# Spectral matrices in their own tiles loaded ahead, two row tiles, and early expert slots taken from three places of the list

## The chip, the cores and the metric

One core of a Trainium2 chip runs the kernel. The metric is the device time of one execution in microseconds (us). Of the kernel before there are three runs, 3310.20, 3313.72 and 3321.25 us; their median is 3313.72 us. Another execution was taken with a profile, 3312.02 us, and every row below is of that one.

## The reference

Eight sequences of 3072 tokens with 256 channels pass a spectral filter, a feed-forward block that takes the largest of three projections, and a mixture of eight experts of which each token uses one. [...]

```python
X = np.fft.rfft(x, axis=1)
x = np.fft.irfft(X * F, n=3072, axis=1).reshape(8 * 3072, 256)
h = np.maximum(np.maximum(x @ w1, x @ w2), x @ w3)          # 768 wide
x = h @ w_out
logits = normalize(x) @ normalize(expert_emb).T / tau        # 8 experts
e = argmax(logits); g = softmax(logits)[e]
out[token] = g * (relu(x[token] @ moe2_w1[e]) @ moe2_w2[e])  # 1024 wide
```

Counted with the reference from its own inputs, experts 0 to 7 get 6555, 2627, 10962, 295, 744, 233, 3084 and 76 tokens. In groups of 256, rounded up, that is 26, 11, 43, 2, 3, 1, 13 and 1, in all 100. From the first seven sequences alone, rounded down, it is 22, 8, 37, 1, 2, 0, 10 and 0, in all 80.

## The kernel before, in words

**Three stretches.** The first (to about 124 us) does the spectral filter of sequence 0 as a pass of its own (`whole`), while the weights of the feed-forward block are decoded from 64-bit words. The second (to about 2118 us) walks 48 units `u` of 512 tokens, six to a sequence. Each unit has 18 ticks `pt`; in each tick TensorE does one group of six 512-column matmuls (`f_group`, tile `p`), in ticks 3 to 6 also the second projection of the unit before (`x2_tile`, tile `pso`), and `fill` puts a piece of the next sequences' spectral passes between them, as a planner with due points says. The third stretch (from 2118 us) does the experts: 100 slots of 256 tokens (`SURE`), one after the other, some 11.45 us each.

**A spectral pass** (class `Pass`) has a stage A, which transforms along one factor and writes to memory, and a stage B of steps `i`. Step `i` consists of two pieces. `b1` loads (`z_load`, `b_load`, on SyncE's queue), splits the input of the next step (`b_split`) and multiplies (`b_fwd`, tile `psb`); `b2` mixes and multiplies back (`b_inv` of step i-3, in the whole pass i-2, tile `psi`). One tile `bt` holds both matrices of a step, forward and inverse, and is kept until `b_inv` has used it; there are five. The filter values `ft` have two tiles, the inputs `x` four. One tick after `b_fwd`, VectorE does the shuffle `t` and the product `u`, and a tick later GpSimd multiplies `t` by the filter.

**Row tiles.** `x2_tile` writes unit u-1's result into one tile `r` (pool `r_p`, one buffer); `x2_store` sends it to memory from SyncE's queue in tick 17, after the last step of `route2` has written the gate into it (L600). `route3` scatters the token numbers into one list per expert (GpSimd, L639).

**Expert slots.** `tables` works out on VectorE which list row each slot takes: `tables(0, 12, ...)` for the first 12 slots (`EARLY`) in unit 43, from the first seven sequences, and `tables(12, ...)` for the rest in the third stretch. Three buffers hold expert weights; slot s uses buffer s modulo 3, and each buffer walks a contiguous run of the list (`_runs`). `w_load(s, i)` (GpSimd's queue, L990) gathers half i of a slot's weights, 2 MB; if the slot's expert is the one that the buffer already holds, its row numbers are out of bounds and nothing is moved. Buffer 2 lies in `wt`, the feed-forward weights, and comes free with the last `f_group`. A slot's tokens are gathered by GpSimd (`x_load`, `xg`), turned by SyncE (`x_turn`, DMA transposes, `xw`), and spread and split on ScalarE and VectorE (`x_split`: L1055, L1056, L204, L205, `xT`).

Of the kernel before, what the change touches and what calls it, by code (L numbers as in the profile page):

```python
# [10 lines left out]
F32 = mybir.dt.float32  # L11
F32R = mybir.dt.float32r
# [11 lines left out]
E, FF = 8, 1024  # L24
# [17 lines left out]
RELEASE = 18 * 38  # L42
NW = 3
# [70 lines left out]
def _runs(n):  # L114

    at = np.arange(128)
    size = (n + NW - 1 - np.arange(NW)) // NW
    start = np.cumsum(size) - size
    return np.where(at < n, start[at % NW] + at // NW, at)

# [6 lines left out]
def _layout(inputs):  # L127
# [11 lines left out]
    c32 = np.zeros((128, 160), np.float32)  # L139
# [5 lines left out]
    c32[:, 26:26 + 128] = np.arange(128)  # L145
    c32[:, 154] = _runs(EARLY)
    c32[:, 155] = _runs(SURE - EARLY)
# [6 lines left out]
        "b32": np.stack([b, bi], 2).astype(np.float32),  # L154
# [15 lines left out]
def fft_filter_maxout_moe_kernel(ctx: ExitStack, tc: tile.TileContext, I, out):  # L170
# [20 lines left out]
    c32 = const.tile([128, 160], F32, name="c32")  # L191
# [4 lines left out]
    pidx, sgn, iotas = c32[:, 24:25], c32[:, 25:26], c32[:, 26:26 + 128]  # L196
    runs = c32[:, 154:155], c32[:, 155:156]
# [9 lines left out]
    def body():  # L207
        st = ExitStack()
        with st:
            def mk(name, bufs, **kw):  # L210
# [7 lines left out]
            b_p, f_p, x_p, xs_p, o_p, u_p, t_p, ys_p = (  # L218
                fft.enter_context(tc.tile_pool(name=n, bufs=b))
                for n, b in (("b", 5), ("f", 2), ("x", 4), ("xs", 3), ("o", 3), ("u", 3), ("t", 3), ("ys", 4))  # L220
# [24 lines left out]
            class Pass:  # L245
# [69 lines left out]
                def b_load(self, i):  # L315
                    if not 0 <= i < self.nb:
                        return
                    if self.whole:
                        bt = b_p.tile([96, 2, 2, 96], F32, tag="b", name="bt")
                        sp.dma_start(out=bt, in_=I["b32"][2 * i:2 * i + 2].rearrange("g p m o -> p g (m o)"))  # L320
                        ft = f_p.tile([96, 2, 2, D], F32, tag="f", name="ft")
                        sp.dma_start(out=ft, in_=I["filt"][2 * i:2 * i + 2].rearrange("g p m o -> p g (m o)"))
                    else:
                        bt = b_p.tile([96, 4, 96], F32R, tag="b", name="bt")
                        sp.dma_start(out=bt.bitcast(F32), in_=bmd[i // 4][i % 4])
                        ft = f_p.tile([96, 1, 2, D], F32, tag="f", name="ft")
                        sp.dma_start(out=ft[:, 0], in_=I["filt"][i])
                    self.t["b", i] = bt
                    self.t["f", i] = ft
# [544 lines left out]

            slot = {}
            cols = {}

# [392 lines left out]
```

## Time and profile before

| what | us |
|---|---|
| median of three runs | 3313.72 |
| the profiled execution | 3312.02 |
| its span, first to last instruction | 3310.1 |
| TensorE matmul busy in the span | 3186.3 |
| VectorE, ScalarE, GpSimd busy | 1916.9, 1527.8, 1245.5 |
| mean granted TensorE clock | 0.98 of full |

The span is 1.9 us shorter than the execution's own time. A row of instructions reads: start, duration (both in us), engine, line, operation, output<-input, count, and in brackets the idle time before it with what ended it. SPq and POOLq are the parts of SyncE and GpSimd that issue. A waits row reads: engine, line, <- what it waited for: us in all, times, longest. A window row reads: stretch, its length, then for PE, PEld, DVE, ACT and POOL the busy time with the count of instructions, the granted clock, the busy share of the DMA engines and GB/s.

### The profile page before, as it was taken

Reading aid. Unit: us, or ns where it says so; the run is one execution under the profiler, and the core shown is the slowest. Engines: PE = TensorE matmul, PEld = TensorE weight load, DVE = VectorE, ACT = ScalarE, POOL = GpSimd, SP = SyncE. Lnnn points to the kernel's source line nnn. Section 1 sums busy time; section 2 is a strip of 40 time slices with the busy share of each in tenths; the row PEclk is TensorE's granted clock in tenths of the full one; section 3 lists DMA queues with packets and bytes.
Section 4 is the critical chain, followed back from the end, with each engine's and each line's share of the span. In section 5 each row is a group of like instructions: output and inputs, shape, how many; then the busy total and the mean of one; then the engine's idle time right before and its main releaser. Section 6 shows DMA issues by size and latency. Waiting matters only on the chain.

```text
span 3310.1 us, 56666 instructions
## 1 busy us (share of the span) xinstructions
PE 3186.3 (96%) x20524; PEld 2858.4 (86%) x20524; DVE 1916.9 (58%) x4249; ACT 1527.8 (46%) x3450; POOL 1245.5 (38%) x1294
## 2 busy tenths in 40 slices
PE   5799999999999999999999999998999999999998
PEld 2588878878788888888888888998999999999998
DVE  7778687677788756878646775542333333333332
ACT  3545545545554554454445554433433333333333
POOL 3233233232233322333322223354555554555553
PEclk6999999999999999999999999999999999999999
DMA  8756566466564452444206777345333457422433
GB/s 247 236 135 141 128 136 138 123 118 151 153 124 101 102 131 89 98 103 98 60 26 174 228 225 216 75 84 160 71 70 69 120 119 186 98 71 70 115 73 93
DMA packets 326911, 409.83 MB, mean 124 GB/s; under 512 B 165784, under 2 KB 234787, under 8 KB 323428
## 3 DMA queue, kind: packets, MB, share of 16 engines
q1 hardware_dynamic: 230324, 247.87, 32.7%
q0 software_dynamic: 55088, 107.96, 11.4%
q10 hardware_dynamic: 41216, 50.35, 4.8%
q8 instruction: 164, 2.69, 0.4%
q14 instruction: 119, 0.97, 0.1%
HBM read 613.68 MB, written 140.97 MB: 228 GB/s over the span
## 4 chain that ended last, share of the span: by engine, by line
PE 55%; issue 19%; POOL 13%; DMA 7%; DVE 4%; ACT 1%; POOLq 1%; SPq 0%; ACTq 0%; DVEq 0%
PE p L201 32%; PE pso L201 13%; POOL out L1099 4%; POOL xg L1035 4%; POOL w L990 4%; PE psi L201 2%; PE psb L201 2%; DMA bt<-bmd 2%; PE psy L201 2%; PE psa L201 2%; POOL wt L990 2%; DMA ft<-in_filt 1%; DMA xw<-xg 1%; DMA s<-ot 1%; PE psh L201 1%
## 5 line engine op out<-in xcount | busy, mean ns | idle before, releaser
L201 PE MATMUL p<-y,wt 128*128 128x512 f32 x5184 | 1322.7, 399 | 1.6 <-DVE m L512 1.0
L201 PEld LDWEIGHTS p<-y,wt 128*128 128x128 f32 x5184 | 954.1, 190 | 206.5 <-DVE m L512 1.5
L1078 DVE SCALAR_TENSOR_TENSOR h<-psh,h 128x512 fp32r<-128x512 f32 x400 | 275.4, 689 | 459.6 <-ACT h L1077 458.0
L201 PEld LDWEIGHTS pso<-wo,h 128*128 128x128 f32 x3456 | 448.6, 189 | 20.4 <-ACT m L508 3.1
L201 PE MATMUL pso<-wo,h 128*128 128x264 f32 x3456 | 454.7, 285 | 2.6 <-ACT m L508 2.6
L201 PE MATMUL psh<-xT,w 128*128 128x256 f32 x3216 | 418.0, 285 | 7.0 <-ACT xT L204 6.6
L201 PEld LDWEIGHTS psh<-xT,w 128*128 128x128 f32 x3216 | 401.8, 193 | 8.0 <-ACT xT L204 7.0
L201 PE MATMUL pso<-w,h 128*128 128x256 f32 x3216 | 407.9, 283 | 0.6 <-ACT o L1094 0.6
L368 POOL TENSOR_TENSOR t<-t,ft 96x256 f32<-96x256 f32 (+1 forms) x176 | 178.3, 1013 | 584.0 <-DVE t L364 285.0
L201 PEld LDWEIGHTS pso<-w,h 128*128 128x128 f32 x3216 | 395.7, 192 | 0.8 <-ACT o L1094 0.8
L1099 POOL DMA_INDIRECT out<-o,ti x200 | 201.8, 1009 | 438.7 <-ACT o L1094 419.7
L1077 ACT ACTIVATE h<-psh 128x512 fp32r<-128x512 f32 x400 | 237.1, 593 | 268.6 <-PE psh L201 268.6
L639 POOL DMA_INDIRECT lst<-ids,pi x192 | 215.1, 1120 | 330.5 <-DVE gs L242 135.7
L486 POOL TENSOR_TENSOR y<-df,sm 128x256 fp32r<-128x256 f32 x192 | 153.1, 798 | 486.8 <-DVE df L485 485.8
L1094 ACT ACTIVATE o<-pso,gate 128x256 f32<-128x256 f32 x200 | 94.8, 474 | 423.3 <-PE pso L201 416.5
L241 ACT ACTIVATE h<-m 128x512 fp32r<-128x512 f32 x288 | 181.4, 630 | 208.9 <-DVE m L516 199.6
L516 DVE TENSOR_TENSOR m<-p,m 128x512 f32<-128x512 f32 x288 | 197.4, 686 | 93.7 <-PE p L201 91.0
L242 DVE TENSOR_TENSOR h<-m,h 128x512 fp32r<-128x512 f32 x288 | 210.0, 729 | 67.1 <-ACT h L241 66.2
L512 DVE TENSOR_TENSOR m<-p,m 128x512 f32<-128x512 f32 x288 | 197.0, 684 | 75.7 <-PE p L201 73.4
L542 ACT COPY r<-pso 128x512 uint16<-128x512 uint16 x192 | 112.5, 586 | 262.9 <-PE pso L201 262.9
L205 DVE TENSOR_TENSOR xT<-xf,xT 128x512 fp32r<-128x512 f32 x100 | 69.3, 693 | 281.6 <-ACT xT L204 278.9
L1035 POOL DMA_INDIRECT xg<-x2d,ti x200 | 208.0, 1040 | 63.9 <-issue 62.8
(158 smaller groups left out, 4199.2 us busy)
## 6 DMA issues: line engine op xcount, KB each, us to landing
wsd<-wsp SPq DMA_DIRECT2D x32, 1024.0 KB, 9.4
ft<-in_filt SPq DMA_DIRECT2D x160, 192.0 KB, 4.5
x2d<-r SPq DMA_DIRECT2D x48, 514.0 KB, 3.3
xt<-in_x SPq DMA_DIRECT2D x96, 256.0 KB, 4.4
s<-ot ACTq DMA_DIRECT2D x96, 256.0 KB, 3.4
gt<-s SPq DMA_DIRECT2D x94, 256.0 KB, 5.0
bt<-bmd SPq DMA_DIRECT2D x160, 144.0 KB, 3.5
raw<-in_e SPq DMA_DIRECT2D x32, 512.0 KB, 6.7
```

The source lines that it names most:

```text
L201: pe.matmul(out=o, lhsT=l, rhs=r, start=start, stop=stop)
L241: act.activation(out=hi, in_=src, func=ACTF.Copy)
L242: later(1, lambda: dve.tensor_tensor(out=lo, in0=src, in1=hi.bitcast(F32), op=ALU.subtract))
L368: later(1, lambda: pool.tensor_tensor(out=t, in0=t, in1=fb, op=ALU.mult))
L512: dve.tensor_tensor(out=m2, in0=ps, in1=m_t[u, fc], op=ALU.max)
L516: dve.tensor_tensor(out=m2, in0=ps, in1=m2, op=ALU.max)
L639: s = pool.indirect_dma_start(out=lst1, out_offset=bass.IndirectOffsetOnAxis(ap=pi[:, t:t + 1], axis=0), in_=ids[:, t:t + 1], in_offset=No ...
L990: pool.indirect_dma_start(out=ws[s % NW][i].bitcast(F32), out_offset=None, in_=wsd[i], in_offset=bass.IndirectOffsetOnAxis(ap=cols["wi"][: ...
L1035: pool.indirect_dma_start(out=g[:, t], out_offset=None, in_=x2d[0:n], in_offset=bass.IndirectOffsetOnAxis(ap=slot[s][:, t], axis=0), bound ...
L1077: act.activation(out=h[:, 0], in_=ps, func=ACTF.Relu)
L1078: dve.scalar_tensor_tensor(out=h[:, 1], in0=ps, scalar=0.0, in1=h[:, 0].bitcast(F32), op0=ALU.max, op1=ALU.subtract,)
L1099: d = pool.indirect_dma_start(out=out, out_offset=bass.IndirectOffsetOnAxis(ap=slot[s][:, t], axis=0), in_=o[:, t], in_offset=None, bounds ...
```

## The change

- **Matrices.** `b_load` becomes `m_load(i, m)` with one tile per matrix: three tiles for forward matrices, loaded two steps ahead, and four for inverse ones, loaded in step i. In the whole pass their memory layout is made contiguous to suit. Filter values get `f_load` and three tiles of one frequency group each (before: two tiles, in the whole pass with two groups each); the whole pass then does two products on VectorE and two on GpSimd where it did one. Inputs are loaded three steps ahead, not two.
- **Rows.** Up to unit 36 odd units have a second row tile, and `x2_store` of a unit moves to tick 3 of the unit after next; later on it stays at tick 17.
- **Slots.** A table `BUF` gives slots 0 to 3 buffers 0, 1, 0, 1, and from slot 4 on all three in turn. Early slots of buffers 0, 1 and 2 take the list from 0, one third and two thirds of its length (5, 4 and 3 slots). `tables` gets the operations for that. Weights are loaded by `AFTER`, the next slot of the same buffer; both halves for slot 4 are issued at the start of slot 0.
- **Small things.** The constants shrink from 160 to 32 columns, and `wT` moves from the tiles `b` to the tiles `t`.

```diff
+TURNS = 36
+def _turns():
+    buf = [0, 1, 0, 1] + [(s + 1) % NW for s in range(4, NSLOT)]
+    num = [buf[at:s].count(buf[s]) for s in range(NSLOT) for at in [0 if s < EARLY else EARLY]]
+    return np.array(buf), np.array(num)
+BUF, NUM = _turns()
+RUN = [int((BUF[:EARLY] == k).sum()) for k in range(NW)]
+BEFORE = [max((i for i in range(s) if BUF[i] == BUF[s]), default=None) for s in range(NSLOT)]
+AFTER = {b: s for s, b in enumerate(BEFORE) if b is not None}
...
-                for n, b in (("b", 5), ("f", 2), ("x", 4), ("xs", 3), ("o", 3), ("u", 3), ("t", 3), ("ys", 4))
+                    ("bf", 3), ("bi", 4), ("f", 3), ("x", 4), ("xs", 3), ("o", 3), ("u", 3), ("t", 3), ("ys", 4),
+                    ("r2", 1),
...
+                def m_load(self, i, m):
+                    p, n = ((bf_p, "bf"), (bi_p, "bi"))[m]
+                    if self.whole:
+                        bt = p.tile([96, 2, 96], F32, tag=n, name="bt")
+                        sp.dma_start(out=bt, in_=I["b32"][m, i])
+                    else:
+                        bt = p.tile([96, 2, 96], F32R, tag=n, name="bt")
+                        sp.dma_start(out=bt.bitcast(F32), in_=bmd[i // 4][i % 4][:, 2 * m:2 * m + 2])
...
+                def f_load(self, i):
+                    gs = range(2 * i, 2 * i + 2) if self.whole else (i,)
+                    for g in gs:
+                        ft = f_p.tile([96, 2, D], F32, tag="f", name="ft")
+                        sp.dma_start(out=ft, in_=I["filt"][g])
...
-                        dve.tensor_tensor(out=u, in0=ps, in1=fa, op=ALU.mult)
+                        for g, ft in enumerate(fts):
+                            w = slice(g, g + 1) if self.whole else slice(0, self.w)
+                            dve.tensor_tensor(out=u[:, w], in0=ps[:, w], in1=by(ft, 0), op=ALU.mult)
...
-                            self.z_load(i + 2)
-                            self.b_load(i + 1)
+                            self.z_load(i + 3)
+                            self.m_load(i + 2, 0)
+                            self.f_load(i + 1)
+                            self.m_load(i, 1)
                             self.b_split(i + 1)
                             self.b_fwd(i)
...
-                        r_p.tile([128, 4, XROW], U16, tag="r", name="r"),
+                        (r2_p if u % 2 and u < TURNS else r_p).tile([128, 4, XROW], U16, tag="r", name="r"),
...
+                    third, thirdi, turn = t8("third", [1]), t8("thirdi", [1], I32), t8("turn", [1])
+                    dve.tensor_scalar(out=third, in0=se[:, E - 1:E], scalar1=21846.0, scalar2=None, op0=ALU.mult)
+                    dve.tensor_copy(out=thirdi, in_=third)
+                    dve.tensor_scalar(out=thirdi, in0=thirdi, scalar1=16, scalar2=None, op0=ALU.logical_shift_right)
+                    dve.tensor_copy(out=third, in_=thirdi)
+                    dve.tensor_scalar(out=turn, in0=run, scalar1=third, scalar2=num, op0=ALU.mult, op1=ALU.add)
...
+                for k in range(NW if at else 0):
+                    yield
+                    lo, ln = t8(f"lo{k}", [1]), t8(f"ln{k}", [1])
+                    mine(lo, cols["lo", k])
+                    mine(ln, cols["ln", k])
+                    dve.tensor_scalar(out=lo, in0=row, scalar1=lo, scalar2=ln, op0=ALU.is_ge, op1=ALU.mult)
+                    dve.tensor_tensor(out=row, in0=row, in1=lo, op=ALU.add)
...
-                    dve.tensor_scalar(out=done, in0=ss, scalar1=-1.0, scalar2=float(n), op0=ALU.mult, op1=ALU.add)
-                    dve.tensor_scalar(out=done, in0=done, scalar1=0.0, scalar2=None, op0=ALU.max)
-                    dve.tensor_tensor(out=done, in0=done, in1=nf, op=ALU.min)
+                    dve.memset(done, 0.0)
+                    for k in range(NW):
+                        first, lo, ln = t8(f"first{k}", [1]), t8(f"elo{k}"), t8(f"eln{k}")
+                        dve.tensor_scalar(out=first, in0=third, scalar1=float(k), scalar2=None, op0=ALU.mult)
+                        for o, off in ((lo, 0), (ln, RUN[k])):
+                            dve.tensor_scalar(out=o, in0=ss, scalar1=-1.0, scalar2=first, op0=ALU.mult, op1=ALU.add)
+                            dve.tensor_scalar(out=o, in0=o, scalar1=float(off), scalar2=0.0, op0=ALU.add, op1=ALU.max)
+                            dve.tensor_tensor(out=o, in0=o, in1=nf, op=ALU.min)
+                        dve.tensor_tensor(out=ln, in0=ln, in1=lo, op=ALU.subtract)
+                        dve.tensor_tensor(out=done, in0=done, in1=ln, op=ALU.add)
+                        cols["lo", k], cols["ln", k] = lo, ln
...
                     if s == first:
-                        w_load(s + 2, 0)
+                        w_load(AFTER.get(s - 1, 4), 0)
+                        w_load(AFTER.get(s - 1, 4), 1)
...
-                            if s + 2 < end:
-                                w_load(s + 2, 1)
-                        if j == 3 and s + 3 < end:
-                            w_load(s + 3, 0)
+                            if s > first and AFTER.get(s - 1, end) < end:
+                                w_load(AFTER[s - 1], 1)
+                        if j == 3 and AFTER.get(s, end) < end:
+                            w_load(AFTER[s], 0)
...
-                    elif pt == 17:
-                        x2_store(u - 1)
+                if pt == 3 and u <= TURNS:
+                    x2_store(u - 2)
+                if pt == 17 and TURNS <= u < 48:
+                    x2_store(u - 1)
```

## Rows read from the trace of the kernel before

**Rows 1.** Windows by stage; the columns are told above.
```profile
33.00:108.00 75.00, 47.03 (x130) 26.89 (x130) 64.93 (x108) 21.15 (x41) 31.03 (x25) 0.66 0.89 236
...
150.00:870.00 720.00, 690.10 (x3903) 593.75 (x3903) 531.06 (x1346) 380.98 (x1021) 217.93 (x259) 0.98 0.59 137
870.00:1110.00 240.00, 234.34 (x1213) 193.02 (x1213) 208.77 (x425) 121.44 (x289) 88.17 (x83) 0.99 0.55 113
...
1950.00:2000.00 50.00, 48.98 (x270) 41.59 (x270) 40.09 (x103) 30.70 (x65) 18.00 (x16) 1.00 0.68 177
...
2160.00:3300.00 1140.00, 1123.72 (x9362) 1122.28 (x9361) 377.03 (x717) 438.28 (x777) 589.72 (x582) 0.99 0.40 100
```

**Rows 2.** Waits of TensorE from 150 to 870 us, the two longest.
```profile
PE psb L201 <- DMA bt<-bmd: 24.0, 9, 3.8
PE psi L201 <- DVE u L366: 4.8, 4, 1.2
```

**Rows 3.** Waits of SyncE's queue from 150 to 1110 us, two of them.
```profile
SPq L325 <- PE psi L201: 355.9, 87, 11.1
SPq L607 <- DVE r L600: 95.8, 11, 20.9
```

**Rows 4.** Chain of waits, two pieces (start, us, what); then the matmul on the timeline.
```profile
228.94 0.40 PE psi L201 x3
...
229.35 8.68 DMA bt<-bmd
...
238.17 0.93 PE L201 MATMUL psb<-zs,bt 96*96 96x256 f32 x3 [3.53 <-DMA bt<-bmd]
```

**Rows 5.** Windows over four gaps of TensorE, two in the second stretch, two in the third.
```profile
234.00:246.00 12.00, 8.47 (x32) 6.75 (x30) 7.66 (x20) 3.68 (x11) 2.41 (x4) 0.72 0.71 156
414.00:426.00 12.00, 8.30 (x39) 6.72 (x38) 8.20 (x22) 4.17 (x11) 2.34 (x4) 0.86 0.64 124
...
2286.00:2306.00 20.00, 9.01 (x59) 8.52 (x58) 4.27 (x8) 3.92 (x7) 5.07 (x5) 0.74 0.63 144
2769.00:2781.00 12.00, 7.72 (x41) 7.22 (x40) 3.14 (x5) 3.89 (x7) 3.44 (x4) 0.72 0.79 189
```

**Rows 6.** Timeline of the whole pass: two loads of filter values, the product between.
```profile
89.62 0.31 SPq L322 DMA_DIRECT2D ft<-in_filt  x1
...
94.47 1.26 POOL L368 TENSOR_TENSOR t<-t,ft 96x512 f32<-96x512 f32 x1 [1.84 <-DMA ft<-in_filt]
...
95.76 0.31 SPq L322 DMA_DIRECT2D ft<-in_filt  x1
```

**Rows 7.** Groups by form: line, engine, operation, count | busy us, mean ns | idle before.
```profile
L368 POOL TENSOR_TENSOR t<-t,ft 96x256 f32<-96x256 f32 x96 | 75.1, 782 | 295.3 <-DVE t L364 126.1 <-issue 124.9 <-DMA ft<-in_filt 24.0
```

**Rows 8.** Timeline of VectorE at the early table: first and last of 11 operations.
```profile
1980.14 0.16 DVE L948 COPY es<-pse 128x12 f32<-128x12 f32 x1
...
1981.66 0.17 DVE L966 TENSOR_TENSOR done<-done,nf 128x8 f32<-128x8 f32 x1
```

**Rows 9.** Waits of TensorE from 2090 to 2170 us (first), then 2170 to 3310 us.
```profile
PE psh L201 <- ACT xT L204: 2.4, 1, 2.4
...
PE psh L201 <- ACT xT L204: 15.0, 2, 10.8
```

**Rows 10.** Windows of the expert stretch: weight loads without and with a wait.
```profile
2267.00:2282.00 15.00, 15.00 (x128) 15.00 (x127) 4.90 (x10) 5.37 (x10) 8.66 (x9) 1.00 0.89 325
2282.00:2297.00 15.00, 5.46 (x46) 5.26 (x44) 0.16 (x1) 0.39 (x2) 1.02 (x1) 0.84 1.09 185
...
2751.00:2776.00 25.00, 20.72 (x167) 20.23 (x167) 6.55 (x13) 7.73 (x14) 9.39 (x10) 0.95 1.05 221
...
3127.00:3147.00 20.00, 20.00 (x170) 20.00 (x169) 6.49 (x11) 8.43 (x15) 9.99 (x10) 1.00 0.89 270
```

**Rows 11.** Timeline at the first slot: a weight load on GpSimd, a spread on ScalarE.
```profile
2116.58 1.08 POOL L990 DMA_INDIRECT wt<-wsd,wi  x1 [11.16 <-PE p L201]
...
2126.50 0.79 ACT L1055 COPY xf<-xw 128x512 uint16<-128x512 uint16 x1 [1.41 <-DMA xw<-xg]
```

More of the change, by code (lines that the diff above doesn't have):

```diff
@@ L144, in _layout @@
     c32[:, 25] = np.where(p % 32 < 16, -1, 1)
-    c32[:, 26:26 + 128] = np.arange(128)
-    c32[:, 154] = _runs(EARLY)
-    c32[:, 155] = _runs(SURE - EARLY)
+    c32[:EARLY, 26] = BUF[:EARLY]
+    c32[:EARLY, 27] = NUM[:EARLY]
+    size = [int((BUF[EARLY:SURE] == k).sum()) for k in range(NW)]
+    at = np.arange(EARLY, SURE)
+    c32[:, 28] = np.arange(128)
+    c32[:SURE - EARLY, 28] = (np.cumsum(size) - size)[BUF[at]] + NUM[at]
     return {
@@ L190, in fft_filter_maxout_moe_kernel @@
     tri = const.tile([128, 2, 128], BF16, name="tri")
-    c32 = const.tile([128, 160], F32, name="c32")
+    c32 = const.tile([128, 32], F32, name="c32")
     tau = const.tile([128, 1], F32, name="tau")
@@ L365, in filt, with rest @@
                         u = u_p.tile([96, self.w, D], F32, tag="u", name="u")
-                        dve.tensor_tensor(out=u, in0=ps, in1=fa, op=ALU.mult)
+                        for g, ft in enumerate(fts):
+                            w = slice(g, g + 1) if self.whole else slice(0, self.w)
+                            dve.tensor_tensor(out=u[:, w], in0=ps[:, w], in1=by(ft, 0), op=ALU.mult)
                         self.t["u", i] = (u, t)
-                        later(1, lambda: pool.tensor_tensor(out=t, in0=t, in1=fb, op=ALU.mult))
+                        def rest():
+                            for g, ft in enumerate(fts):
+                                w = slice(g, g + 1) if self.whole else slice(0, self.w)
+                                pool.tensor_tensor(out=t[:, w], in0=t[:, w], in1=by(ft, 1), op=ALU.mult)
+                        later(1, rest)
                     later(1, filt)
@@ L740, in aug_steps @@
                 yield
-                wT = b_p.tile([128, 2, 128], F32, tag="b", name="wT")
+                wT = t_p.tile([128, 2, 128], F32, tag="t", name="wT")
                 act.copy(out=wT, in_=ps)
@@ L903, in tables @@
                 dve.tensor_scalar(out=lastv, in0=se[:, E - 1:E], scalar1=-1.0, scalar2=None, op0=ALU.add)
+                if at:
+                    turn = turns
+                else:
[5 more added lines that the diff above has]
+                    dve.tensor_scalar(out=turn, in0=run, scalar1=third, scalar2=num, op0=ALU.mult, op1=ALU.add)
                 yield
-                if done is not None:
-                    dve.tensor_tensor(out=cnt, in0=ss, in1=done, op=ALU.subtract)
-                else:
-                    dve.tensor_copy(out=cnt, in_=ss)
                 sm, ge, eid, sel, st0, row = (
@@ L948, in tables @@
                 dve.tensor_copy(out=es, in_=ps[:, 0:n])
-                if at:
-                    dve.tensor_tensor(out=sf, in0=es, in1=cols["es"][:, at - NW:at + n - NW], op=ALU.is_equal)
-                else:
-                    dve.tensor_tensor(out=sf[:, NW:], in0=es[:, NW:], in1=es[:, :n - NW], op=ALU.is_equal)
-                    dve.memset(sf[:, 0:NW], 0.0)
+                dve.memset(sf, 0.0)
+                i = 0
+                while i < n:
+                    b = BEFORE[at + i]
+                    j = next((j for j in range(i, n) if b is None or BEFORE[at + j] != b + j - i), n)
+                    if b is not None:
+                        ea = cols["es"]
+                        dve.tensor_tensor(out=sf[:, i:j], in0=ea[:, at + i:at + j], in1=ea[:, b:b + j - i], op=ALU.is_equal)
+                    i = max(j, i + 1)
                 wf = m2_p.tile([128, n], F32, tag="m2", name="wf") if at else t8("wf", [n])
```

73 lines of the change are left out of this document (33 added, 40 removed).

## The prediction

> **What bounds the kernel now.** I read the windows by stage first [rows 1]. TensorE is the bound nearly everywhere: from 870 to 1110 us it is busy 234.34 of 240, among the experts 1123.72 of 1140. So the time to be won is where it isn't: 75 - 47 = 28 us in the pass of sequence 0, 720 - 690.1 = 29.9 us from 150 to 870, and 16.3 us among the experts. Then TensorE's waits say who ends those gaps. In the second stretch 24.0 of the 29.9 us end with the load of the spectral matrices, nine waits of up to 3.8 us [rows 2]. Among the experts 2.4 + 15.0 = 17.4 us end with `xT`, three waits in all [rows 9], so the input of a slot is late, not its weights. In the first pass TensorE follows others: VectorE is busy 64.93 of 75 us.
>
> Why is the matrix load late? SyncE's queue tells it: its loads of `bt` waited 355.9 us for `psi`, 87 times [rows 3]. One of them was issued at 229.35, at once after a `psi` (the one at 228.94), landed 8.68 us later, and the `psb` that wanted it had been idle from 234.64 (238.17 - 3.53) [rows 4]. So five tiles that stay taken until the inverse product give the load 5.3 us, about one and a half steps.
>
> [...]
>
> **The change, part by part.** All terms are made against the profiled execution, 3312.0 us; the median 3313.7 is 1.7 us above it, and about 10 us (0.3%) is what a measurement can tell from no change.
>
> *Matrices ahead, second stretch.* A forward tile is now free once `b_fwd` three steps earlier is done; the load therefore has three steps, twice 5.3, about 10.6 us, against the 8.68 us of a slow landing. The inverse tile has more still. The 24.0 us of waits should go. With them goes the low clock: two gaps like the first window of rows 5, three like the second, (1 - 0.72) x 12 = 3.4 and (1 - 0.86) x 12 = 1.7 us each, 2 x 3.4 + 3 x 1.7 = 11.9 us of TensorE's time. Some of that lies inside the gap itself, so I take 8; the stretch's own 0.98 allows 0.02 x 720 = 14 [rows 1]. Next late are the products on VectorE, `psi` on `u`, 4.8 us now [rows 2]; they stay. VectorE has room: 531.06 us in what would be some 690 is 77%, and it is 87% busy from 870 to 1110, where TensorE still reaches 97.6% [rows 1]. I keep 2 us for landings still slower. **Term: -24 - 8 + 2 = -30**, bounds -38 (24 + 14) and -10 (a third of it, if another wait takes the place).
>
> The 160 more issues on SyncE cost nothing as long as its queue waits for tiles for hundreds of microseconds [rows 3]; if that cover goes, `gt` and `zt`, queued behind, come late. The move of `x2_store` takes 95.8 us of waiting for the gate (L600) off the same queue up to unit 36 [rows 3], and the loads queued behind it with it. No wait of TensorE in rows 2 names those loads, so I count nothing for it; the second row tile is what lets the store be late. The step from tile `b` to tile `t` for `wT` and the shorter constants count nothing either: a few small operations beside TensorE's work.
>
> *The whole pass.* Here the change takes away as well as gives. Two filter tiles of two groups become three of one, one and a half steps in flight, not two. Now the loop is: issue at 89.62, product at 94.47 (4.85 us later), product done after 1.26, next issue in that tile at 95.76 [rows 6]; 6.14 us for two steps, 3.07 each. With three tiles, three products of about 0.78 us [rows 7] come per 4.85 + 0.78 + 0.03 = 5.66 us, one and a half steps, 3.77 us each: 0.7 more where this loop binds. The 16 steps take 75 us, 4.7 on average, so about the last half is bound so: 8 x 0.7 = 5.6. Fewer bytes in flight shorten the landing somewhat. **Term: +4**, bounds +11 (all 16 steps) and -10 (VectorE's idle time in the stage, 75 - 64.93, if the deeper loads of inputs and matrices fill it).
>
> *The early table.* I count 4 operations more in its first part and 26 more in one run later. Eleven such now go from 1980.14 to 1981.83, 0.154 us each [rows 8]: 30 x 0.154 = 4.6 us of VectorE in which the maxima of `p` queue. TensorE idles 1.02 us in that window as it is [rows 1]. It has five buffers of products to go on with, so **+2**, bounds 0 and +4.6. The late table's additions lie where VectorE is busy 377 of 1140 us: nothing.
>
> *The slots.* From the counts, the list before puts expert 0 into all 12 early slots; from slot 12 on buffer 1 goes to expert 2 at slot 13 and buffer 2 at slot 14, later changes are at slots 41, 47, 54, 56, 59, 87 and 98. TensorE's waits lie on just these: the window 2267 to 2282 carries 325 GB/s of weights, and in the next TensorE works 5.46 of 15 us [rows 10], the 10.8 us of rows 9; the other is at 2751 to 2776, slots 54 and 56, 4.28 us; slot 87 at 3127 to 3147 costs nothing, 20.00 of 20 [rows 10], and so 41, 47, 59 and 98. The wait of 2.4 is that for slot 3, beside the second half of slot 2's weights. With the new order buffer 0 holds expert 0, buffer 1 expert 1, buffer 2 expert 2, and go on so: changes at slot 12 alone (buffer 1 to expert 2), then 40, 46, 55, 58, 77, and **97 and 98, again neighbours**. The three waits go, 17.4 us, and with them the low clock, 0.26 x 20 + 0.28 x 12 = 8.6 us over the two larger, mostly inside the waits, so I take 5: -22. The pair at the end is issued exactly as the pair at 13 and 14 was; the nearest row is that one, so I put back 10.8 + 2 = 13 (bounds 0 and 13).
>
> At slot 0 both halves for slot 4 are issued together, once `wt` is free (2116.58, after 11.16 us of waiting [rows 11]); the second half was issued later before. Queued behind on GpSimd are small things that wait for VectorE anyway. But `xw` of slot 1 is turned beside it, and ScalarE waited 1.41 us for it already [rows 11]. A half moves in 5 to 6 us (325 GB/s, 2 MB), so this wait may grow by 5; the projections of unit 47 hide most of it: +1.5 (0 to 5). **Term: -22 + 13 + 1.5 = -7.5**, bounds -22 and 0.
>
> Sum: -30 + 4 + 2 - 7.5 = -31.5; 3312.0 - 31.5 = **3280 us**.
>
> [...] The windows show the engines busy 0.89 with 325 GB/s while two halves pass, and the turned inputs late behind it [rows 10]. [...]
>
> **The rivals.**
> (1) *The pair at the end costs nothing.* For it: in 2282 to 2297 the engines are busy 1.09 and move only 185 GB/s, in 2751 to 2776 1.05 and 221, whereas five other changes passed without [rows 10]; so a slow spell of the DMA, not the order, may have made the two waits, and it need not come again at 97. Against: the pair is the only one of its kind and it waited. Time: 3280 - 13 = 3267.
> (2) *The matrix wait is replaced.* All loads stand in one queue and land in the same slow spells; the inputs, the filter or ScalarE's stores may be next. Then a third of the 30 is won: 3280 + 20 = 3300. Against: nothing but `u`, 4.8 us, is seen waiting besides.
> (3) *Slower: the filter loop of the whole pass.* If a landing takes longer there than 4.85 us, three tiles bind all 16 steps: (landing + 0.78) / 1.5 each, against 4.7 now. The other terms are -35.5; the time is 10 us over the median once a step takes 4.7 + 47 / 16 = 7.6 us, a landing of 10.7 us. At 12 us it is 8.5 a step, +61, 3338 us. For it: the engines are 0.89 busy there [rows 1], and landings of 8.68 occur [rows 4]. Against: 4.85 us is with more bytes in flight than after.
> That the change doesn't do what it says, the loads issued no earlier for another tile's sake, ends as (2).
>
> **How the numbers follow.** Forecast 0.50, rival (1) 0.22, (2) 0.16, (3) 0.06, and 0.06 for what I have not seen. The likeliest is 3280. From 3256 (rival 1 with the full -38 of the matrices) to 3303 (rival 2 and a little) holds 8 in 10. Faster by over 0.3% is below 3303.8: 0.50 + 0.22 + two thirds of (2), 0.11, together 0.83; within 0.3%: 0.05 of (2) and 0.04, 0.09; slower: 0.06 and 0.02, 0.08.
>
> **What would show it.** Waits of `psb` for `bt` gone or under 5 us from 150 to 870 us, the clock there at 1.00, and that stretch's work done some 30 us earlier; steps of the whole pass 3.5 to 3.8 us apart at its end; no wait of TensorE at slots 3, 13 and 14, one of about 10 us at slot 98; ScalarE waiting longer than 1.41 us for slot 1's `xw`. It is wrong if the waits of `psb` persist under another name, if the whole pass grows by over 11 us, or if the slots lose time where the order has no change of expert.

## The result, and the profile after

The changed kernel takes 3256.36 us (median of four runs, 3255.01 to 3258.55), the kernel before 3311.96 us (four runs): a ratio of 0.9828, 95% interval 0.9807 to 0.9848. That is 56 us less; the forecast was 32 less. The profiled execution took 3255.0 us, its span 3253.2.

By stage first, the windows of the changed kernel; the columns are those of [rows 1].

```profile
33.00:108.00 75.00, 49.56 (x115) 28.68 (x116) 57.54 (x119) 19.27 (x38) 35.41 (x39) 0.55 0.76 211
150.00:870.00 720.00, 702.38 (x3991) 605.95 (x3989) 545.24 (x1385) 391.38 (x1051) 220.66 (x263) 0.99 0.59 141
1950.00:2000.00 50.00, 45.73 (x232) 38.53 (x231) 41.10 (x132) 24.95 (x52) 18.51 (x17) 0.93 0.70 166
2310.00:2710.00 400.00, 400.00 (x3474) 400.00 (x3474) 141.66 (x252) 164.24 (x290) 220.14 (x218) 1.00 0.39 93
```

Beside the last line, the same stretch of the kernel before, a row that the prediction did not look at:

```profile
2310.00:2710.00 400.00, 400.00 (x3355) 400.00 (x3354) 133.00 (x245) 158.25 (x280) 212.86 (x210) 1.00 0.37 91
```

These two lines hold most of the surprise. Both kernels show TensorE busy for all of 400 us, both at a granted clock of 1.00; one does 3355 products in that time and the other 3474, 119.2 against 115.1 ns each. The tiles and the number of products of a slot are the same. So a slot without any wait takes 11.06 us after and 11.46 before.

Then the waits of TensorE, after, from 150 to 870 us, and among the experts from 2110 us on:

```profile
PE psi L213 <- DVE u L389: 16.1, 9, 2.5
PE psb L213 <- issue: 1.1, 5, 0.3
```

```profile
PE psh L213 <- DMA w<-wsd,wi: 4.2, 1, 4.2
PE psh L213 <- ACT xT L216: 1.0, 1, 1.0
PE pso L213 <- ACT o L1159: 0.6, 1, 0.6
```

The nine waits of `psb` for the matrices [rows 2] are gone, but nine of `psi` for `u`, 4.8 us in four before, are 16.1. Among the experts the three waits for `xT` of 17.4 us [rows 9] are down to 1.0, and there is a new one for weights. Two more readings, the waits of TensorE from 1900 to 2030 us, where the early table is worked out, and the one of ScalarE for slot 1's turned tokens (1.41 us in [rows 11]):

```profile
PE p L213 <- DVE m L550: 2.4, 1, 2.4
PE p L213 <- DVE m L546: 1.8, 1, 1.8
```

```profile
ACT xf L1120 <- DMA xw<-xg: 6.2, 1, 6.2
```

Where the 56.9 us between the two spans lie is best read from the starts of TensorE's products: the first `p` of units 0, 22, 43 and 45, and the first `psh` of each slot. The table gives the lengths in between (us; the first column is a point of time), worked out from those starts.

| kernel | unit 0 at | 0 to 22 | 22 to 43 | 43 to 45 | 45 to slot 0 | slots 0-3 | 13, 14 | 54, 55 | 97, 98 | other 89 |
|---|---|---|---|---|---|---|---|---|---|---|
| before | 123.7 | 989.7 | 821.1 | 73.5 | 110.5 | 53.9 | 36.2 | 30.3 | 22.9 | 1019.6 |
| after | 133.5 | 970.1 | 821.1 | 80.2 | 110.9 | 56.1 | 22.1 | 22.1 | 24.1 | 984.8 |
| difference | +9.8 | -19.6 | 0 | +6.7 | +0.4 | +2.2 | -14.1 | -8.2 | +1.2 | -34.8 |

The last column, slots with no change of expert and next to no wait, was in no term of the sum. (The last slot's length is not in the table.)

### The profile page after: what moved, and what is told of

It reads as the page before. It is cut to its first block, busy times and chain, and to the rows that moved or that the text cites. A ratio compares the mean times of both kernels' runs of the same rounds, so it can differ in the third digit from the quotient of the medians.

```text
span 3253.2 us, 57237 instructions
## 1 busy us (share of the span) xinstructions
PE 3152.3 (97%) x20524; PEld 2824.1 (87%) x20524; DVE 1932.0 (59%) x4313; ACT 1527.2 (47%) x3450; POOL 1249.9 (38%) x1310
## 4 chain that ended last, share of the span: by engine, by line
PE 58%; issue 6%; POOL 4%; DMA 2%; DVE 2%; ACT 0%; POOLq 0%; SPq 0%; ACTq 0%; DVEq 0%
PE p L213 21%; PE pso L213 20%; PE psh L213 12%; PE psy L213 1%; PE psi L213 1%; PE psb L213 1%; POOL out L1164 1%; POOL xg L1100 1%; POOL w L1055 1%; PE psa L213 1%; DMA gt<-s 1%; DMA w<-wsd,wi 1%; DMA xw<-xg 1%; POOL wt L1055 0%; DMA wt<-wsd,wi 0%
## 5 line engine op out<-in xcount | busy, mean ns | idle before, releaser
L213 PE MATMUL psh<-xT,w 128*128 128x256 f32 x3264 | 406.2, 279 | 5.9 <-DMA w<-wsd,wi 4.2
L213 PE MATMUL pso<-w,h 128*128 128x256 f32 x3264 | 400.3, 278 | 0.6 <-ACT o L1159 0.6
L213 PEld LDWEIGHTS psh<-xT,w 128*128 128x128 f32 x3264 | 389.8, 189 | 6.8 <-issue 4.3
L213 PEld LDWEIGHTS pso<-w,h 128*128 128x128 f32 x3264 | 388.1, 188 | 0.8 <-ACT o L1159 0.8
```

The costliest lines, as they stand in the source:

```text
L213: pe.matmul(out=o, lhsT=l, rhs=r, start=start, stop=stop)
```

## The experiments

**Does the pace of the slots hang on where the tiles lie?** The change moved some tiles. The constants shrank by 128 columns, which is 512 bytes and so nothing modulo 512; `xT`, `h` and `wt` kept their places. The additional small tiles of `tables`, allocated ahead of the two weight buffers `w0` and `w1`, moved these by 64. The places as allocated, in bytes per partition modulo 512, with what the window from 2310 to 2710 us of each run gave (400 us over the products in it):

| run | xT and h | w0, w1 | wt | ns per product |
|---|---|---|---|---|
| before | 320 | 320 | 384 | 119.2 |
| after | 320 | 384 | 384 | 115.1 |
| e1 | 320 | 448 | 384 | 117.9 |
| e2 | 320 | 384 | 384 | 115.2 |
| e3 | 256 | 384 | 384 | 118.6 |
| e5 | 384 | 448 | 384 | 118.0 |
| e6 | 320 | 416 | 384 | 118.0 |

My theory was that the weight buffers' place sets the pace; the rival was the new order of slots. The first two runs put one unused tile of 64 bytes ahead of `w0`, in the changed kernel (e1) and in the kernel before (e2):

```diff
+                    k_p.tile([128, 16], F32, name="gap")
                     w0 = ws_p.tile([128, 8192], F32R, name="w0")
```

> The changed kernel with one unused tile of 64 bytes per partition allocated ahead of the first expert weight buffer: both gathered weight buffers start at 64 instead of 0 modulo 128 bytes, as in the kernel before; nothing else differs. Theory (start address sets the pace of TensorE among the experts): from 2310 to 2710 us about 3355 matmuls instead of 3474, a slot 11.43 to 11.5 us instead of 11.06, the whole 3256 + 37 = 3293 us. Rival (the new order of buffers and slots, or the 512 bytes by which everything else moved, sets the pace): 3474 matmuls, 3256 us.

> The kernel before with the same unused tile of 64 bytes ahead of the weight buffers: they start at 0 modulo 128 bytes. Theory (start address): some 3475 matmuls in 400 us of undisturbed slots, slots of 11.06 us, 3312 - 37 = 3275 us, with the waits of the second stretch and at slots 13, 14, 54 and 56 as they were. Rival (order, or the 512 bytes): 3312 us.

e1: 3277.0 us; e2: 3286.9 us, where the kernel before took 3316.2 on the same chip. Two windows, of e1 and of e2:

```profile
2310.00:2710.00 400.00, 400.00 (x3392) 400.00 (x3391) 135.04 (x248) 160.56 (x284) 214.44 (x212) 1.00 0.37 91
```

```profile
2310.00:2710.00 400.00, 400.00 (x3473) 400.00 (x3472) 143.70 (x255) 163.35 (x289) 219.58 (x216) 1.00 0.38 93
```

The old order with the new places has the new pace, 3473 products; its 89 quiet slots take 985.4 us. The new order with other places loses most of it. So it is the places. e1 returned 21 of the 37 us that I expected, as 64 bytes more is not the old place but a third one. The waits in e2 stayed those of before (`psh` for `xT` 18.7 us), so without the pace the change is worth 26 to 31 us by the medians: 55.6 less the 29.2 that e2 won, or 3286.9 - 3256.4; the runs of e2 lie between 3278 and 3294.

Is it the weights alone, or where they lie against the other operand? e3 moves the activations (the tile `ent` that stood ahead of them goes behind them), e5 moves activations and weights, e6 moves the weights by 32 bytes only.

```diff
-                ent = wp.tile([128, 2, E], F32, name="ent")
+                ent = ent_p.tile([128, 2, E], F32, name="ent")
...
+            wp.tile([128, 16], F32, name="gap2")
...
+                    k_p.tile([128, 8], F32, name="gap")
                     w0 = ws_p.tile([128, 8192], F32R, name="w0")
```

The first two lines are e3, the third is e5, the last two are e6.

> The changed kernel with the one tile of 64 bytes that stands ahead of the activations (y, gs and xT, h, o) moved behind them: these start at 0 instead of 64 modulo 128 bytes; the weight buffers stay at 0. Theory (any operand of TensorE that starts at 64 costs 3.5 per cent): a second stretch some 3 per cent shorter and slots under 11.06 us, as far as 3190 us. Rival (only weights, or only the operand that is out of step with the others, matter): 3256 us, within 5. Second rival (what counts is that both operands differ modulo 128): slower by 30 to 100 us.

> The changed kernel with an unused tile of 64 bytes per partition ahead of everything that holds activations: xT and h start at 0 modulo 128 bytes, the two gathered weight buffers at 64, the third (wt) at 0 as before. Theory (a matmul runs slower when both its operands start at the same place modulo 128 bytes, whichever): products with the gathered buffers at 114.7 to 117 ns from one start to the next, those with wt at 118 to 120, slots of 11.1 to 11.3 us, 3256 + 5 to 20 us. Rival (weight buffers at 64 are slow by themselves): products with the gathered buffers at 118.5 to 120 ns, with wt at 115 to 118, 3277 us or more.

> The changed kernel with an unused tile of 32 bytes ahead of the gathered weight buffers, which start at 32 modulo 128 bytes where xT and h start at 64 (wt at 0). Theory one (only the same start is slow): 114.7 to 117 ns from product to product, 3256 us. Theory two (only a distance of 64 is fast): products with the gathered buffers at 118 to 120 ns, with wt at 115 to 118, 3275 to 3280 us.

e3: 3282.8 us, e5: 3257.8, e6: 3282.8. e3 keeps all the weights where they were and is slow like e1, so the weights' own place is not it. The groups of products by operands in the same 400 us (count, busy, mean ns of one) show it per buffer, of the kernel before and of e5:

```profile
L201 PE MATMUL psh<-xT,w 128*128 128x256 f32 x1140 | 146.5, 283 | 0.0
L201 PE MATMUL pso<-w,h 128*128 128x256 f32 x1099 | 139.5, 283 | 0.0
L201 PE MATMUL pso<-wt,h 128*128 128x256 f32 x576 | 71.8, 279 | 0.0
L201 PE MATMUL psh<-xT,wt 128*128 128x256 f32 x540 | 69.2, 281 | 0.0
```

```profile
L213 PE MATMUL psh<-xT,w 128*128 128x256 f32 x1114 | 140.5, 281 | 0.0
L213 PE MATMUL pso<-w,h 128*128 128x256 f32 x1123 | 138.8, 279 | 0.0
L213 PE MATMUL psh<-xT,wt 128*128 128x256 f32 x576 | 75.0, 283 | 0.0
L213 PE MATMUL pso<-wt,h 128*128 128x256 f32 x576 | 73.0, 283 | 0.0
```

Before, `w` lies at the same place as `xT` and `h` (283 ns) and `wt` 64 bytes on (279 to 281). In e5 it is the other way round, and so are the times. In the changed kernel all three buffers lie 64 on, and all groups read 278. 128 apart (e1, e3) gives 281, 96 apart (e6) 280 to 282. For these products of 256 columns the same place is the slowest and 64 apart the fastest of those tried. But a product doesn't go by its own pair alone: from start to start, pairs 64 apart take 114.7 to 115.7 ns in the changed kernel and up to 117.9 in runs whose other products are slower (117.8 and 117.9 before, 116.8 and 117.4 in e5).

In e5 the second stretch was faster as well: units 22 to 43 in 810.1 us, against 821.1 in all kernels above but e3 (819.7). There `y` had come to the place of `wt` (both 384; 320 in the changed kernel, 256 in e3). e9 moves `y` alone, by allocating it between `wt` and `wo`.

```diff
-            wp = mk("wp", 1)
-            g_p, gs_p, y_p, sm_p = mk("g", 3), mk("gs", 2), mk("y", 2), mk("sm", 2)
+            wp, y_p, wo_p = mk("wp", 1), mk("y", 2), mk("wo", 1)
+            g_p, gs_p, sm_p = mk("g", 3), mk("gs", 2), mk("sm", 2)
```

> The changed kernel with the tiles y allocated between wt and wo: they start at 384 modulo 512 bytes as wt does, instead of 320; xT, h and the gathered weights keep their places modulo 512. Theory (the place of y against wt sets the pace of the 512-column products, the same place being the fast one there, as in the run with the activations moved by 64): units 36 to 43 take 35.34 us each instead of 35.96, slots stay at 11.06 to 11.17, 3256 - 47 x 0.6 = 3228 us. Rival (the gain of that run came from h against wo or gs against cm): 35.9 us a unit, 3256 us.

> The changed kernel once more, unchanged, on the chip of the other three. If the pace of the slots goes by the places of the tiles: 11.06 or 11.17 us a slot, 3256 us within 8. If it falls out by chance in each execution: anything from 11.06 to 11.5, 3256 to 3295 us. First product of unit 0 at 130 to 134 us, unit 0 to 22 in 964 to 970 us.

e9: 3236.0 us, ratio to before 0.9766 (0.9744 to 0.9787); e12, the changed kernel beside it: 3253.6 us, 0.9817 (0.9796 to 0.9839). Units 22 to 43 take 810.4 against 821.1, slots 11.06 in both. A window in that stretch, of e12 and of e9:

```profile
1700.00:1900.00 200.00, 200.00 (x1102) 171.43 (x1101) 132.43 (x276) 109.00 (x230) 48.99 (x56) 1.00 0.65 189
```

```profile
1700.00:1900.00 200.00, 200.00 (x1127) 174.78 (x1127) 133.28 (x271) 115.75 (x248) 50.14 (x57) 1.00 0.69 195
```

Here the same place is the fast one, 1127 products in 200 us against 1102: with products of 512 columns it is the other way round, so no one rule came out, only that the place of the operands counts. e12 also shows that the pace is no accident of one execution: of nine profiled runs with the places of the changed kernel (e2, e4, e7 to e12 and the changed kernel itself, all on chips where the kernel before took 3305 to 3323 us) eight settled on 11.06 us a slot and e4 on 11.17; e2 ran at 11.17 too until the wait at slot 13, and at 11.06 after it.

So the time of a product hangs on start addresses: only these differ between e2 and the kernel before, and a product takes 115.2 or 119.2 ns. What makes it so, no run here shows.

**The pass of sequence 0.** The first product of unit 0 came 9.8 us later. It is at 123.7 and 128.8 us in the two profiles with the old pass (before, e2) and at 130.1 to 134.8 in eleven with the new one, mean 132.9, so 132.9 - 126.3 = 6.6 us is the measured size, roughly, as the two old ones lie 5 us apart. e4 has four filter tiles of one group, e8 two of two groups as before.

```diff
-                    ("bf", 3), ("bi", 4), ("f", 3), ...
+                    ("bf", 3), ("bi", 4), ("f", 4), ...
...
-                        ft = f_p.tile([96, 2, D], F32, tag="f", name="ft")
+                        ft = f_p.tile([96, 2, 2, D], F32, tag="f", name="ft")
```

The last two lines are of e8, which has `("f", 2)`.

> The changed kernel with four filter tiles of one group instead of three: as many bytes of the filter in flight as the kernel before had. Theory (three tiles give the pass of sequence 0 only one and a half steps in flight, which cost it 9.8 us): the first product of unit 0 at 124 to 127 us instead of 133.5, and 3247 to 3250 us. Rival (the deeper loads of inputs and matrices, queued ahead of the filter on SyncE, or the two products in place of one, cost it): the first product of unit 0 at 132 to 134 us, 3256 us.

> The changed kernel with the filter tiles of the kernel before: two tiles, in the pass of sequence 0 of two groups each, so one product on VectorE and one on GpSimd per step again; the order of loads stays new. Theory (two products in place of one cost the pass of sequence 0 its time, since four tiles of one group gave back only 2.9 us): first product of unit 0 at 124 to 127 us instead of 133.5. Rival (the order of the loads on SyncE costs it): 130 to 134 us. The filter of the other passes has two tiles too; theory: second stretch within 3 us of the changed kernel.

e4: 3256.9 us and 130.6, near the lower edge of the eleven; e8: 3262.5 us and 128.5. The last seven steps of the pass (starts of `psb`, steps 8 to 15) took 22.1 us in both old profiles, 25.8 to 27.7 in the eleven, 24.7 in e4 and 23.3 in e8: the tiles are a part of it, but single profiles that scatter so much don't say how large a part. In e8 the second stretch got slower, 973.1 us for units 0 to 22.

**The second stretch, the early table, the slots' start.** e7 undoes the second row tile and the moved store, and spreads the early table's new sums; e10 makes three edits in three stretches, e11 adds the place of `y`; e14 asks for the inputs a step earlier.

```diff
-TURNS = 36
+TURNS = 0
...
                         cols["lo", k], cols["ln", k] = lo, ln
+                        yield
```

> Two edits of the changed kernel in stretches of their own. Up to unit 36 one row tile, stored in tick 17 of the next unit, as before the change. The early table's new sums per buffer are spread over three ticks more. Theory for the first (the matrices alone give the second stretch its 20 to 26 us, the rows nothing): first product of unit 0 to that of unit 22 takes 964 to 970 us as in the changed kernel, waits of psb for bt still gone. Rival (the store's wait for the gate held up the loads behind it): 980 to 990 us, with new waits of psi or psb. Theory for the second (26 operations of VectorE in one run hold up the maxima): unit 43 to unit 45 takes 74 to 76 us instead of 80. Rival (the sums themselves, wherever they are): 80.

e7: 3254.3 us. Units 0 to 22 took 966.6 us, within the changed kernel's 963.6 to 970.1 (it, e1, e3, e4, e6 and e12): the row tiles give nothing, the matrices and the inputs all of it. Units 43 to 45 fell from 80.2 to 75.4 us, but from unit 45 to slot 0 went 117.4 us instead of 110.9, with a wait of `p` on GpSimd's `y` (2.5 us) and a granted clock of 0.95 from 2000 to 2040 us. So the burst moved and the loss with it; what the table takes from TensorE isn't undone by spreading it over three ticks. The forecast of 74 to 76 us for units 43 to 45 came, and the time did not.

```diff
-                    ("bf", 3), ("bi", 4), ("f", 3), ...
+                    ("bf", 3), ("bi", 6), ("f", 2), ...
...
-                    if s == first:
-                        w_load(AFTER.get(s - 1, 4), 0)
-                        w_load(AFTER.get(s - 1, 4), 1)
+                            if s == 2:
+                                w_load(4, 1)
...
+                        if j == 3 and s == 1:
+                            w_load(4, 0)
```

> Three edits of the changed kernel in stretches of their own. (1) Pass of sequence 0: two filter tiles of two groups and the order and depth of loads of the kernel before (inputs two steps ahead, both matrices one step ahead). Theory (filter tiles and order together cost it 6 us): first product of unit 0 at 124 to 128 us; rival (the split of the matrices in two loads): 130 to 133. (2) Six tiles of inverse matrices instead of four. Theory (SyncE's queue waits for psi before it can issue the inputs behind, so zt is late): waits of psi for u from 150 to 870 us fall from 13 to 16 us to under 5 and unit 0 to 22 takes 955 us instead of 964 to 970; rival (slow spells of the transfers themselves): 12 to 16 us still, 964 to 970. (3) Both halves of slot 4's weights issued at the end of slot 1 and in slot 2, not at the start of slot 0. Theory (slot 2's empty load stands behind them on GpSimd's queue): the step from slot 1 to slot 2 takes 11.1 to 11.6 us instead of 15.9; rival: 15 to 16. All three by theory 3256 - 5 - 11 - 5 = 3235 us.

> The three edits and the place of y together: by the theories 3256 - 21 - 28 = 3207 us; if only y holds, 3228; if only the three edits hold, 3235; if neither, 3256.

e10: 3255.6 us, e11: 3234.4; beside e12 (3253.6) and e9 (3236.0) the three edits together win nothing that can be told. (1) Unit 0 began at 132.1 and 129.8, not at 124 to 128: nothing for the theory, and where the rest of the 6.6 us goes stays open. (2) `psi` waited 14.3 us for `u` (14.6 in e11), as with four tiles: the rival. The length of the stretch can't be used here, as e10 has the two filter tiles of e8 and took 973.3 us like it. (3) The step from slot 1 to slot 2 took 13.0 and 13.5 us instead of 15.7 to 16.1: about half; slots 0 to 3 take 49.8 and 52.1 us instead of 55.1 (e12), but slot 4 takes 12.7 and 11.7 instead of 11.1.

```diff
-                    ... ("x", 4), ...
+                    ... ("x", 5), ...
...
-                            self.z_load(i + 3)
+                            self.z_load(i + 4)
```

> The changed kernel with five input tiles instead of four and the inputs of stage B asked for four steps ahead instead of three. Theory (an input that lands late holds ScalarE's and VectorE's queues, so that psb's space comes free late and psi waits): waits of psi for u from 150 to 870 us fall from 14 to 16 us to under 6, unit 0 to 22 takes 952 to 960 us instead of 964 to 970. Rival (VectorE's own queue, full in these ticks with the steps of route2, makes them): 12 to 16 us still, 964 to 970.

`psi` waited 13.2 us for `u`, nine times: the theory of late inputs falls too. How such a wait looks in the changed kernel, a part of the timeline up to 428 us:

```profile
416.83 0.37 SPq L350 DMA_DIRECT2D ft<-in_filt  x1
...
423.44 0.35 ACT L320 COPY ot<-psi 96x256 f32<-96x256 f32 x1
...
426.14 0.31 ACTq L321 DMA_DIRECT2D s<-ot  x1
...
426.50 0.42 ACT L256 ACTIVATE zs<-zt 96x256 fp32r<-96x256 f32 x1 [2.71 <-DMA bt<-bmd]
...
426.95 0.42 DVE L257 TENSOR_TENSOR zs<-zt,zs 96x256 fp32r<-96x256 f32 x1 [1.19 <-ACT zs L256]
...
427.30 0.44 DVE L385 STREAM_SHUFFLE t<-psb 96x256 f32<-96x256 f32 x1
...
427.63 0.41 DVE L389 TENSOR_TENSOR u<-psb,ft 96x256 f32<-96x256 f32 x1
...
428.10 0.60 PE L213 MATMUL psi<-ys,bt 96*96 96x256 f32 x3 [2.47 <-DVE u L389]
```

ScalarE stands 2.71 us before the split `zs`, VectorE stands behind it with the other half of that split, only then takes `psb` out of its space, and `psi` needs that space. It is always in the tick in which `route2` runs. The line names a load of matrices, but the semaphore events of the trace say more: ScalarE's queue is held ahead of the split, at the issue of the store of `ot` (L321). The store carries the same completion semaphore as the filter load above, issued at 416.83; the last part of that load landed at 426.07, and the queue went on at 426.09. It is so in all six waits of `psi` over 1.2 us (12.6 of the 16.1 us): each time the queue went on 0.02 us after the last landing of an `ft` load issued 7.5 to 9.2 us earlier. The other three waits are of 1.2 us each, as the four before the change were. The change asks for the matrices 12.8 us (median) ahead of their product, 7.2 before, but for the filter values only 7.7 us, 6.2 before. No run asked for the filter values a step earlier, so that this would win the 12.6 us is not shown.

**Does each product go by its own operands, and does it hold on other chips?** e13 is e9 with `ent` behind `gs`, so that `xT` alone lies 128 from the weights; e15 is e9 with the inputs four ahead and slot 4's weights late. e16 and e17 repeat them, e18 is the changed kernel.

```diff
-            g_p, gs_p, sm_p = mk("g", 3), mk("gs", 2), mk("sm", 2)
+            g_p, gs_p, ent_p, sm_p = mk("g", 3), mk("gs", 2), mk("ent", 1), mk("sm", 2)
```

> As the run with y in step with wt, but the tile of 64 bytes that lay behind wo now lies behind gs: xT starts at 256 modulo 512 bytes, 128 from all three weight buffers; h stays at 320, 64 from them. Theory (each product's pace goes by its own two operands): psh at 118 to 120 ns from start to start, pso at 115 to 118, slots of 11.2 to 11.3 us, 3236 + 12 to 25 us. Rival (one pace for the sequence, set by any pair): psh and pso alike, both at 114.7 to 116 or both at 118 to 120.

> The place of y, the inputs four ahead, and slot 4's weights asked for late, together: by all three theories 3236 - 9 - 3 = 3224 us; without the inputs 3233; with neither 3236.

> As e13. On a chip where the kernel before takes 3305 to 3323 us: by the theory (each product by its own operands) psh at 118 to 119 ns, pso at 115 to 118, a slot of 11.2 to 11.35 us, some 3236 + 20 = 3256 us; by the rival (one pace for all) both near 115 or both near 119, 3236 or 3270 us. On a chip like the last one: slots of 11.8 us again.

> As e15. Where the kernel before takes 3305 to 3323 us: slots of 11.06 to 11.17 us, the step from slot 1 to slot 2 at 11.1 to 12.3 instead of 15.9, waits of psi for u 13 to 16 us still, 3230 to 3236 us. On a chip like the last one 3303 to 3313.

> The changed kernel again. If the 11.77 us a slot belong to the chip: on one like the last, slots of 11.7 to 11.8 and some 3325 us; on another, slots of 11.06 to 11.17 and 3253 to 3258 us. If they belong to the edits of e13 to e15: 11.06 to 11.17 here, and 11.77 in e16 and e17 beside it.

The runs e13 to e18 fell on two other chips, on which the kernel before took 3348.2 and 3340.3 us. Measured: e13 3313.9, e14 3327.6, e15 3308.3; e16 3305.2, e17 3301.2, e18 3319.8 us. From start to start `psh` takes 118.7 to 118.9 ns in e13 and e16 and 115.4 to 115.8 in the other four, `pso` 117.7 to 117.8 against 115.8 to 116.6: the product whose operand moved is the one that slows down most, as each going by its own operands would have it; the other one slows down by 1 to 2 ns too, which that theory alone doesn't give.

In e15 and e17 the step from slot 1 to slot 2 took 12.2 and 12.3 us, and `psi` waited 15.3 and 14.7 us for `u`.

But a slot takes 11.67 to 11.78 us (medians) in all six, the changed kernel (e18) among them. Its waits of TensorE there, from 2300 us on:

```profile
PE pso L213 <- ACT o L1159: 25.5, 71, 0.6
PE psh L213 <- ACT xT L216: 3.8, 1, 3.8
```

And a slot of e12, then one of e18, the first half's evacuation `o` behind its product:

```profile
2506.28 1.58 PE L213 MATMUL psh<-xT,wt 128*128 128x256 f32 x12
2506.49 0.47 ACT L1159 ACTIVATE o<-pso,gate 128x256 f32<-128x256 f32 x1 [2.12 <-PE pso L213]
```

```profile
2500.90 1.58 PE L213 MATMUL psh<-xT,wt 128*128 128x256 f32 x12
2502.29 0.47 ACT L1159 ACTIVATE o<-pso,gate 128x256 f32<-128x256 f32 x1 [3.14 <-PE pso L213]
...
2502.82 3.09 PE L213 MATMUL pso<-w,h 128*128 128x256 f32 x24 [0.34 <-ACT o L1159]
```

On the one chip `o` starts 0.2 us after TensorE has gone on to `psh`, on the other 1.4 us, and the second half of `pso` waits for it in nearly every slot. It starts 2.0 to 2.1 us (medians) after the issue of the slot's second weight load (`w_load`, which moves nothing: from 2310 to 2510 us of the changed kernel's profile 37 such loads are issued, in full 74 MB, and all queues together move 14.5 MB) in all six runs, 0.8 us in the changed kernel's profile; why, these rows don't show. In e18 the step from `psh` to that half takes 0.60 us from start to start, 0.12 in e12, and the next one 0.22: together 0.59 of the 0.62 us by which a slot is longer. On those chips the change is worth 3340.3 - 3319.8 = 20.5 us, a ratio of 0.9938 (0.9912 to 0.9963), and the pace of the products counts less.

## Why the prediction was right and wrong

The direction was right. What it did count came near its 31.5 us only by luck: without the pace the change is worth 26 to 31 us by the medians with e2, but 18 by the two profiled executions (56.9 less 34.8 and the 4 of the pace in the other slots), and each term behind it was off. The forecast as a whole was too small by the pace.

**The step that failed** is the first: "TensorE is the bound nearly everywhere ... So the time to be won is where it isn't [busy]", with the experts' stretch put down at 16.3 us. Busy 1123.72 of 1140 us [rows 1] was read as full speed. TensorE was busy and still took 119.2 ns a product where 115.1 was to be had: a place of tiles that the change moved as a side effect was worth 34.8 us over 89 quiet slots, and another 11 us per 21 units lay in `y`, which the change left alone. The prediction had no term for where a tile lies. Of the small parts it looked at the shorter constants, which indeed move nothing modulo 512; the small tiles of `tables`, which moved the weights by 64, it counted as operations only.

**Matrices: -30, measured -19.6 (in five other runs -21 to -26).** The waits for `bt` went, as worked out. The part that failed is "Next late are the products on VectorE ... they stay": the filter loads, which the change asks for only one step ahead as before, landed as late as before (3.1 us after their issue in the median and up to 10.6, before 3.2 and 10.6), held ScalarE's queue at its stores, and 16.1 us stood under the name of `u` where 4.8 had. That is rival (2), which names the filter and ScalarE's stores, with two thirds won instead of one. "It is wrong if the waits of `psb` persist under another name" was the right thing to look at.

**The whole pass: +4, measured about +6.6.** The steps at its end were forecast 3.77 us apart; the last three came 3.83 apart here and 3.25 to 3.87 in the ten other profiles. The filter's loads landed sooner, as the forecast had it: 3.2 us after their issue (median of 32 loads of 192 KB) against 4.7 before (16 of 384 KB). The filter loop was not the only thing that counted: the first two steps were faster (3.9 us against 5.7), the next three slower (6.1, 6.9 and 7.8 against 4.6, 4.1 and 6.4), which no term had.

**The early table: +2 (0 to 4.6), measured +6.7.** The bound left out what a gap does to the clock, which the same text counts elsewhere. The record of the granted clock has 0.5 of full for 3.4 us at each of the two waits of `p` on VectorE (1.8 and 2.4 us), 0.93 over 50 us, which is up to 3.5 us more, some of it inside the waits. Not every gap does this: in the kernel before, from 150 to 870 us, five of TensorE's eight gaps of 2.3 to 3.8 us had 0.5 of full beside them, for 3.4 or 6.8 us, and three of 2.3 to 2.5 us had not.

**The slots' waits: -7.5, measured -18.9** (+2.2 - 14.1 - 8.2 + 1.2, the pace in it 4). The three waits went. For slot 1's `xw` ScalarE waited 6.2 us, 1.41 before; the forecast was 5 more (though 2 MB at 325 GB/s take 6.2 us, not 5 to 6), and TensorE lost 0.35 of it. What it did not see is slot 2: its load moves nothing, but stands behind both halves for slot 4 on GpSimd's queue, and TensorE waited 4.2 us for it; with these halves asked for later (e10, e11) that step was 2.2 to 3.2 us shorter, which bears it out for about half. The last wait, put back with 13, took 24.1 - 2 x 11.06 = 2.0 us here. In the twelve runs on the first chips with the new order it took 0 to 2 us in five and 6 to 8 in seven, so the pair does cost at its new place, about half of what was put back, and not always: rival (1) and the forecast each hold in part. The old pair took 13.3 us in the kernel before and 19 in e2. What makes the pair cost in some runs and not in others, no run shows.

**Rival (3)** did not come: the whole pass grew by 6 to 10 us, not by 61.

## What to carry to other kernels

A share of busy time near 100% at full clock doesn't say that an engine is at its best (here 400 of 400 us at a granted clock of 1.00 held 3355 products before and 3474 after): divide the window by the count of instructions, and compare that with another stretch or another kernel. When an edit adds or shrinks any tile, look at where the operands of the hot products have moved to, and try two or three places on purpose; here one pool moved in the code gave 17.6 us (3253.6 to 3236.0) and 64 bytes 21 to 29. When one load of a step is moved ahead, ask which of the step's other loads is then the last, here the filter's, with 12.6 us of waits. And a load that moves nothing can be as late as the loads ahead of it on its queue: TensorE waited 4.2 us for that of slot 2, and 1.6 and 2.1 us where those ahead were asked for later (e10, e11).

## What the runs showed of the hardware that I had not expected

- A product's time hangs on where its two operands start: 278 ns in the mean where all lie 64 bytes apart modulo 512, 283 at the same place (256 columns); for 512 columns the same place is the faster, 38.6 us a unit against 39.1 (units 22 to 43).
- The same places can settle on two paces, 11.06 and 11.17 us a slot, and e2 went from one to the other at the wait of slot 13.
- ScalarE's queue stood at a store until the last part of a filter load on SyncE's queue, with the same completion semaphore, had landed: 2.71 us at 426 us, released 0.02 us after the landing.
- Two of the experiments' five chips ran the same slots at 11.67 to 11.78 us, where one small operation of ScalarE started 1.2 us later in each; the wait for it is 0.59 of the 0.62 us in e18.
